# Batch-sized token groups, a ring for the GELU outputs, and a new order of all operations

## The chip, the cores and the metric

The kernel runs on one core of a Trainium2 chip. The time is what the device takes for one execution, in microseconds; before the change the median of three runs is 363.52 us (363.21 to 363.70).

## The reference

Squared-ReLU attention with 8 batches, 12 heads, 448 tokens and 64 elements per head is followed by a two-layer network over all 3584 tokens:

```python
scores = scale * np.matmul(q, k.transpose(0, 1, 3, 2))      # 1/sqrt(64)
attn = np.maximum(scores, 0.0) ** 2 / S
x = np.matmul(attn, v).transpose(0, 2, 1, 3).reshape(B * S, H * D)   # 3584 x 768
h = x @ w_in                                                 # 768 x 2048
g = h * (1.0 / (1.0 + np.exp(-1.702 * h)))                   # GELU
return (g @ w_out).astype(np.float32)                        # 2048 x 768
```

## The kernel before

Everything on the matrix engine is in float16 with float32 sums. The whole kernel is a list of some 1950 short words (lines 467 to 640), each of which issues one operation; `do` (line 441) translates them one after the other. The order of the words is the order of every engine's queue. Nothing else plans the work. A word is a letter, its indices, after `:` the engine (`a` ScalarE, `d` VectorE, `p` GpSimd), and after `@` the accumulator banks of PSUM that it takes. There are eight banks, each a pool of its own with one buffer, so a word that takes a bank waits until the last reader of that bank is done.

**Attention.** Four heads of a batch make a unit; there are 24 units, three to a batch. k and q of units 0 to 5 are brought in by GpSimd's queue (words `jk`, `jq`, which also narrow to float16) or by SP's (`Lk0`, `Lq0`) and turned around on TensorE (`tk`, `tq`, line 126, evacuated by `ek`, `eq`). Later units are loaded by SP (`Lk`, `Lq`), narrowed (`K`, `Q`) and turned around by a transposing DMA on SP's queue (`Rk`, `Rq`, line 117). v always comes over GpSimd's queue (`V`). A score word `s` (line 143) issues four quadrant products of 64 x 64 weights over 448 columns, and each unit has seven. Two ReLUs `r` and one square `x` follow it, on ScalarE or VectorE. When all seven are done, `a` (line 173) issues 28 quadrant products with v, and words `e` (line 189) copy the result into the transposed activations `xts`.

**First layer.** Tokens are taken in eight groups, `gblk = [6, 8] * 4` blocks of 64: 384 and 512 tokens in turn. Two batches of seven blocks make one pair of groups, so a batch's result is split between two groups, and `e` has pieces of 384, 64 and 448 columns. Group 0 is done plainly, by words `f` (line 221, two products each, 96 products in all) with GELU `g` and a widening `v` after it. The other groups use a scheme of seven products instead of eight (Strassen-Winograd) for each of four units of the 2048 hidden columns: words `u` (line 269, six products each, over half the group's tokens). `T` and `S` make the sums of activations and weights, `t` copies a first sum out of PSUM, `b` adds to it, `g` is the GELU and `v` the widening, mostly on GpSimd, into the outputs `gts`. These have one buffer for groups of even number (`ge`) and one for odd (`go`). The float32 tiles between `t` and `v` come from pool `gf`, which has five buffers.

**Second layer.** It works on tiles of 128 tokens. Two neighbouring tiles of a group make a pair, again with seven products instead of eight: words `p` (line 377), eight products of 384 columns each. `A` (line 357) makes the sums of activations, partly in place in `gts`; `W` made those of the weights once. `h` copies a partial result out, `l` adds the last part, `o` stores a tile in two pieces over SP's queue. A group of 512 tokens has two pairs. One of 384 has a pair and an unpaired tile, done by two words `i` (line 399, 16 products each) and copied out by `n`. Both of the last pair's tiles are stored in quarters by words `q`, on SP's and ScalarE's queues.

Before the first data arrive, 14 products with zeros run on TensorE (`z`), the first after two memsets on VectorE.

Of the kernel before, what the change touches and what calls it, by code (L numbers as in the profile page):

```python
# [15 lines left out]
def kernel(  # L16
# [22 lines left out]
    WO = 8  # L39

    gblk = [6, 8] * (B // 2)
    gcum = [0]
    for n in gblk:
        gcum.append(gcum[-1] + n)
    NG = len(gblk)
# [6 lines left out]
    for name, bufs in (("cst", 1), ("kst", 1), ("qst", 1), ("k16", 2), ("q16", 2), ("v16", 4),  # L52
                       ("kT", 3), ("qT", 3), ("at", 11), ("xe", 1), ("xo", 2),
                       ("T1", 1), ("T2", 1), ("T4", 1), ("ge", 1), ("go", 1), ("gf", 5),
                       ("as0", 1), ("as1", 1), ("osb", 3)):
        pool(name, bufs)
# [15 lines left out]
    wT = [const(f"wT{n}", [128, WO, NOUT]) for n in range(3)]  # L72

# [115 lines left out]
    def xt_evac(e, p, u, n, s):  # L189
        b, pr = divmod(u, NP)  # L190
        lo = b * J
        for _ in range(n + 1):
            g = max(i for i in range(NG) if gcum[i] <= lo)
            hi = min((b + 1) * J, gcum[g + 1])
            at, lo = lo, hi
        if g not in xts:
            xts[g] = new("xe" if g % 2 == 0 else "xo", [128, NK, 64 * gblk[g]], F16)
        copy(e, xts[g][:, 2 * pr + s, 64 * (at - gcum[g]):64 * (hi - gcum[g])],
             units[u]["av"][s][:, 64 * (at - b * J):64 * (hi - b * J)])
# [6 lines left out]
    gts = {}  # L206

    def gt_of(g):
        if g not in gts:
            gts[g] = new("ge" if g % 2 == 0 else "go", [128, NF, 64 * gblk[g]], F16)  # L210
        return gts[g]
# [9 lines left out]
    def m1(e, p, g, f, r):  # L221
        n = 64 * gblk[g]
        if r == 0:
            hp[g, f] = bank(p, "ht")
        w = win[f // WQ]
        fo = (f % WQ) * 128
        for i in (2 * r, 2 * r + 1):
            nc.tensor.matmul(out=hp[g, f][:, 0:n], lhsT=w[:, i, fo:fo + 128],  # L228
                             rhs=xts[g][:, i, 0:n], start=i == 0, stop=i == NK - 1)
# [3 lines left out]
    def m1_gelu(e, p, g, f):  # L233
        n = 64 * gblk[g]
        gfs[g, f] = new("gf", [128, 512], F32)
        gelu(gfs[g, f][:, 0:n], hp.pop((g, f))[:, 0:n])

    def m1_widen(e, p, g, f):
        n = 64 * gblk[g]
        widen(e, gt_of(g)[:, f, 0:n], gfs.pop((g, f))[:, 0:n])  # L240
# [11 lines left out]
    def x_block(g, kh, th):  # L252
        hn = 32 * gblk[g]
        return xts[g][:, kh * HK:(kh + 1) * HK, hn * th:hn * th + hn]
# [4 lines left out]
    def t_sum(e, p, g, n):  # L259
# [6 lines left out]
        xsum[g, n] = new(f"T{n}", [128, HK, 256], F16)[:, :, 0:32 * gblk[g]]  # L266
        tt(xsum[g, n], x, y, ALU.subtract, e)

    def unit_product(e, p, g, i, n):
        hn = 32 * gblk[g]  # L270
# [9 lines left out]
        for t in range(2):  # L280
            mm(hx[g, i, c][:, t * hn:(t + 1) * hn],
               lambda j: a[:, j, t * 128:(t + 1) * 128], lambda j: b[:, j, :], HK,
               n in (0, 1, 3) and t == 0)

    def half_of(x, g):
        return x[:, 0:64 * gblk[g]]

    def unit_snap(e, p, g, i, n):
        gfs[g, i, n] = new("gf", [128, 512], F32)
        copy(e, half_of(gfs[g, i, n], g), half_of(hx[g, i, 0], g))  # L290
# [4 lines left out]
    def unit_add(e, p, g, i, n):  # L295
        t = half_of(gfs[g, i, unit_tile[n]], g)
        tt(t, half_of(hx[g, i, 1], g), t, ALU.add)

    def unit_gelu(e, p, g, i, n):
        if n == 5:  # L300
            gfs[g, i, 5] = new("gf", [128, 512], F32)
            gelu(half_of(gfs[g, i, 5], g), half_of(hx[g, i, 0], g))
        else:
            t = half_of(gfs[g, i, unit_tile[n]], g)
            gelu(t, t)

    def unit_widen(e, p, g, i, n):
        fh, th = unit_place[n]
        hn = 32 * gblk[g]
        f = WQ * i + 2 * fh  # L310
        widen(e, gt_of(g)[:, f:f + 2, th * hn:(th + 1) * hn],
              half_of(gfs.pop((g, i, unit_tile[n])), g).rearrange("p (t c) -> p t c", t=2))
# [5 lines left out]
    def out_tile(g, m):  # L318
        if (g, m) not in osb:
            osb[g, m] = new("osb", [128, DM], F32)  # L320
        return osb[g, m]

    def store(e, p, g, m):
        t = osb.pop((g, m))
        for i in range(2):
            b, j = divmod(gcum[g] + 2 * m + i, J)
# [3 lines left out]
    def store_part(e, p, g, m, h, i):  # L330
        b, j = divmod(gcum[g] + 2 * m + i, J)
        r0 = b * S + j
        c = slice(h * NOUT, (h + 1) * NOUT)
        (nc.scalar if e == "a" else nc.sync).dma_start(
            out=out[r0:r0 + 63 * J + 1:J, c], in_=osb[g, m][64 * i:64 * i + 64, c])

    def m2(e, p, g, m, h):
        op[g, m, h] = bank(p, "op")
        mm(op[g, m, h][:, 0:NOUT], lambda f: gts[g][:, f, m * 128:(m + 1) * 128],
           lambda f: wout[h][f // WO][:, f % WO, :], NF, True)  # L340

    def m2_out(e, p, g, m, h):
        copy(e, out_tile(g, m)[:, h * NOUT:(h + 1) * NOUT], op.pop((g, m, h))[:, 0:NOUT], 1.0 / SC)
# [8 lines left out]
    def part(g, m, i):  # L352
        return gts[g][:, i * HF:(i + 1) * HF, m * 128:(m + 1) * 128]
# [3 lines left out]
    def a_sum(e, p, g, m, n):  # L357
        a11, a12 = part(g, m, 0), part(g, m, 1)
        if n == 5:
            sums[g, m, 5] = new(f"as{p.pop(0)}", [128, HF, 128], F16, "asum")  # L360
            tt(sums[g, m, 5], a11, a12, ALU.add, e)
            return
        a21, a22 = part(g, m + 1, 0), part(g, m + 1, 1)
        if n in (1, 2):
            sums[g, m, n] = new(f"as{p.pop(0)}", [128, HF, 128], F16, "asum")
        if n == 1:
            tt(sums[g, m, 1], a21, a22, ALU.add, e)
        elif n == 2:
            tt(sums[g, m, 2], sums[g, m, 1], a11, ALU.subtract, e)
        elif n == 3:  # L370
            tt(a21, a21, a11, ALU.subtract, e)
        else:
            tt(a12, a12, sums[g, m, 2], ALU.subtract, e)

    def pair_product(e, p, g, m, n):
        c = (0, 1, 0, 1, 0, 0, 1)[n]
        if n < 2:
            op[g, m, c] = bank(p, "ox")
        a = (lambda: part(g, m, 0), lambda: part(g, m, 1), lambda: sums[g, m, 2],
             lambda: sums[g, m, 1], lambda: part(g, m + 1, 0), lambda: part(g, m + 1, 1),  # L380
             lambda: part(g, m, 1))[n]()
        w = (wout[0][0], wout[0][1], wT[1], wT[0], wout[1][0], wT[2], wout[1][1])[n]
        mm(op[g, m, c][:, 0:NOUT], lambda f: a[:, f, :], lambda f: w[:, f, :], HF,
           n in (0, 1, 3))

    def pair_snap(e, p, g, m, n):
        i, c = {0: (0, lo), 2: (0, hi), 4: (1, hi)}[n]
        copy(e, out_tile(g, m + i)[:, c], op[g, m, 0][:, 0:NOUT], 1.0 / SC)

    def pair_last(e, p, g, m, n):  # L390
        i, c = {1: (0, lo), 3: (1, hi), 5: (1, lo), 6: (0, hi)}[n]
        o = out_tile(g, m + i)[:, c]
        if n == 5:
            copy(e, o, op[g, m, 0][:, 0:NOUT], 1.0 / SC)
        else:
            nc.vector.scalar_tensor_tensor(out=o, in0=op[g, m, 1][:, 0:NOUT], scalar=1.0 / SC,
                                           in1=o, op0=ALU.mult, op1=ALU.add)

    def single(e, p, g, m, h):
        op[g, m, h] = bank(p, "os")  # L400
        o = op[g, m, h][:, 0:NOUT]
        a1, a2 = part(g, m, 0), part(g, m, 1)
        s, t = ((a1, wout[0][0]), (a2, wout[0][1])) if h == 0 else (
            (a1, wout[1][0]), (sums[g, m, 5], wout[1][1]))
        mm(o, lambda f: s[0][:, f, :], lambda f: s[1][:, f, :], HF, True)
        mm(o, lambda f: t[0][:, f, :], lambda f: t[1][:, f, :], HF, False)
# [16 lines left out]
    with tc.manual_schedule():  # L423
        two = {"S": s_sum, "W": w_sum, "T": t_sum, "s": scores, "r": relu, "x": square,
               "e": xt_evac, "f": m1, "m": m2, "o": store, "u": unit_product,
               "t": unit_snap, "b": unit_add, "A": a_sum, "p": pair_product, "h": pair_snap,
               "l": pair_last, "i": single, "n": m2_out, "q": store_part, "jo": load_w_out, "a": attn_v,
# [24 lines left out]

        nc.vector.memset(warm, 0.0)
        nc.scalar.activation(out=warm, in_=warm, func=AF.Gelu_apprx_sigmoid)
        zero = wT[2][:, 0, :]
        nc.vector.memset(zero, 0.0)
        zp = []

        def zeros(e, p, n):
# [8 lines left out]
            "jq1 jk1 V0 z13@0 Lk0 K0:d z1 I tk0@1 Lq0 Q0:d jk3 ek0:a tq0@2 tq1@3 jq3 eq0 eq1 "  # L468
            "s0.1@4.5 r0.1.1 r0.1.0:d s0.4@6.7 r0.4.1:d jq2 s0.6@0.1 r0.6.0:d r0.4.0 V1 r0.6.1 "
            "s0.3@2.3 r0.3.1:d tk1@5 ek1:a s0.0@4.7 r0.0.0 x0.1 s1.4@0.6 r1.4.0:d r0.3.0 r1.4.1 "  # L470
            "s0.2@1.3 r0.0.1 r0.2.0:d s0.5@5.4 r0.5.1:d r0.2.1 r0.5.0 s1.1@0.2 jk2 x0.3 x0.2 "
            "s1.0@6.7 r1.0.1 x0.0 tk3@1 r1.1.1 r1.1.0 jwa0 jwb0 x0.5 x1.4 r1.0.0 s1.5@4.3 x0.4 jwb2 "
            "tq3@5 jq4 r1.5.1 s1.2@7.2 s1.6@0.6 r1.5.0 x1.0 x0.6:a eq3 jk4 V2 jwa2 a0@3.4 r1.6.1:d "
            "tk2@5 ek3 r1.6.0 ek2 x1.1:a tq2@6 eq2 r1.2.1 r1.2.0 e0.0.1:a s1.3@1.0 x1.2 x1.6 jwa1 "
            "r1.3.1 jwb1 s2.3@5.6 s2.1@2.7 e0.1.1:a r1.3.0 x1.3 x1.5 r2.3.0 jk5 jq5 r2.1.1:d e0.0.0 "
            "s2.2@0.4 r2.3.1 r2.2.0 r2.2.1 a1@1.5 s3.0@7.6 x2.3:a e1.0.0:a r2.1.0:d V3 s2.0@0.4 "
            "e1.1.0 r2.0.0 e0.1.0 s2.6@2.1 jwb3 r3.0.0:d r3.0.1 s2.4@0.3 r2.6.0:d f0.3.0@7 f0.2.0@6 "
# [193 lines left out]
```

## Time and profile before

| what | value |
|---|---|
| median of three runs | 363.52 us |
| the profiled execution's own time | 364.18 us |
| its span, first to last instruction | 362.4 us |
| TensorE busy | 352.5 us, 3598 products |
| VectorE busy | 309.1 us, 585 instructions |
| ScalarE busy | 284.9 us, 560 instructions |
| GpSimd busy | 111.8 us, 165 instructions |
| mean granted TensorE clock | 0.999 |
| DMA moved | 51.39 MB |

The page gives each engine's busy time, then the span in 40 slices with tenths of busy time, then the chain of work that ended last, followed back from the last instruction. Names like `hx<-win` are written tile and read tile: `sc` are scores, `av` attention results, `ht` and `hx` first-layer sums of group 0 and of the others, `ox` and `os` second-layer sums of pairs and of unpaired tiles, `tr` transposes, `zp` the zero products. Most products of both layers are issued by one helper (line 203), so that its line says little and the tile names say more. A line of the chain in order of time reads: start, length, engine and tile, and how many instructions were merged.

### The profile page before, as it was taken

The numbers are of one execution on the slowest core, as the hardware profiler recorded it, in microseconds if no ns is written. First come the engines' busy times: TensorE is split into PE (matmuls) and PEld (weight loads), VectorE is DVE, ScalarE is ACT, GpSimd is POOL, SyncE is SP. The second block draws the span as 40 slices with busy tenths as digits, with TensorE's granted clock in tenths as the row PEclk, the third lists the DMA queues.
The fourth block names the chain that finished last, engine by engine and source line by source line (L and its number), as shares of the span: only waits on it lengthen the run. The fifth ranks groups of instructions, "written<-read, shape, count | busy, mean of one in ns | idle before, by whom it ended". The sixth has DMA issues, their size and how long they took to land.

```text
span 362.4 us, 9114 instructions
## 1 busy us (share of the span) xinstructions
PE 352.5 (97%) x3598; PEld 236.0 (65%) x3598; DVE 309.1 (85%) x585; ACT 284.9 (79%) x560; POOL 111.8 (31%) x165
## 2 busy tenths in 40 slices
PE   8789999999999999999999999999999999999995
PEld 4445558855579555886569855786559855678662
DVE  3999999999997999888999799868999789875643
ACT  3999996999989997779996899878897697445420
POOL 5744522354225440155014440165021311001200
PEclk9999999999999999999999999999999999999999
DMA  8999999479999989535893764874590233003124
GB/s 182 173 200 201 215 231 228 107 149 220 196 209 189 241 158 260 165 110 79 203 213 77 216 81 118 147 152 104 115 171 4 47 110 89 2 0 89 44 67 110
DMA packets 65228, 51.39 MB, mean 142 GB/s; under 512 B 35744, under 2 KB 61856, under 8 KB 65184
## 3 DMA queue, kind: packets, MB, share of 16 engines
q1 hardware_dynamic: 48256, 36.32, 42.2%
q0 software_dynamic: 16608, 14.09, 27.0%
q8 instruction: 28, 0.46, 0.6%
q10 hardware_dynamic: 320, 0.39, 0.4%
q14 instruction: 16, 0.13, 0.1%
HBM read 45.61 MB, written 11.01 MB: 156 GB/s over the span
## 4 chain that ended last, share of the span: by engine, by line
PE 90%; DMA 5%; DVE 2%; POOL 1%; issue 0%; ACT 0%
PE hx L203 32%; PE ox L203 31%; PE sc L150 9%; PE av L181 8%; PE os L203 6%; DMA q<-in_q_dram 3%; PE ht L228 3%; DMA k<-in_k_dram 2%; PE zp L463 1%; PE tr L131 1%; DVE at L88 1%; POOL wout L415 0%; DVE at L161 0%; POOL q L104 0%; POOL v L104 0%
## 5 line engine op out<-in xcount | busy, mean ns | idle before, releaser
L163 ACT ACTIVATE at<-sc 128x448 f16<-128x448 f32 x218 | 108.2, 567 | 10.7 <-PE sc L150 9.9
L161 DVE TENSOR_SCALAR at<-sc 128x448 f16<-128x448 f32 x118 | 69.5, 614 | 3.6 <-PE sc L150 3.2
L203 PEld LDWEIGHTS <-win 128*128 128x128 f16 x672 | 61.5, 98 | 8.4 <-issue 1.8
L88 DVE TENSOR_TENSOR at<-at 128x896 f16<-128x896 f16 x109 | 65.9, 633 | 0.9 <-ACT at L163 0.2
L217 POOL TENSOR_SCALAR go<-gf 128x512 f16<-128x512 f32 x42 | 28.2, 671 | 109.9 <-ACT gf L214 108.3
L88 DVE TENSOR_TENSOR gf<-hx,gf 128x512 f32<-128x512 f32 (+1 forms) x84 | 51.6, 627 | 11.0 <-ACT gf L79 7.9
L214 ACT ACTIVATE gf<-gf 128x512 f32<-128x512 f32 (+1 forms) x84 | 47.5, 587 | 13.2 <-DVE gf L88 11.8
L169 ACT ACTIVATE at<-at 128x896 f16<-128x896 f16 x59 | 56.5, 974 | 1.1 <-DVE at L161 0.8
L217 POOL TENSOR_SCALAR ge<-gf 128x384 f16<-128x384 f32 x52 | 29.3, 563 | 73.3 <-ACT gf L214 60.8
L150 PE MATMUL sc<-qT,kT 64*64 64x448 f16 x672 | 48.9, 358 | 2.6 <-DVE qT L83 0.9
L203 PEld LDWEIGHTS <-winS 128*128 128x128 f16 x504 | 46.1, 98 | 5.5 <-issue 0.9
L79 ACT ACTIVATE gf<-hx 128x512 f32<-128x512 f32 (+1 forms) x63 | 34.5, 554 | 18.5 <-PE hx L203 15.0
L203 PE MATMUL ox<-wout,go 128*128 128x384 f16 x256 | 46.3, 326 | 0.0
L203 PEld LDWEIGHTS <-go 128*128 128x128 f16 x320 | 30.1, 98 | 22.0 <-issue 4.3
L203 PE MATMUL hx<-T,winS 128*128 128x256 f16 (+1 forms) x336 | 39.9, 261 | 0.0
L181 PE MATMUL av<-at,v 64*64 64x448 f16 x672 | 36.8, 350 | 0.9 <-ACT gf L214 0.6
L203 PEld LDWEIGHTS <-ge 128*128 128x128 f16 x256 | 24.0, 98 | 18.4 <-issue 4.5
L203 PE MATMUL hx<-xo,win 128*128 128x256 f16 x288 | 35.9, 273 | 0.0
L203 PE MATMUL ox<-wT,asum 128*128 128x384 f16 x192 | 34.9, 327 | 0.0
L150 PEld LDWEIGHTS <-kT 64*64 64x64 f16 x672 | 17.6, 105 | 24.7 <-issue 18.0
L203 PEld LDWEIGHTS <-asum 128*128 128x128 f16 x224 | 21.0, 98 | 15.7 <-issue 2.8
L181 PEld LDWEIGHTS <-v 64*64 64x64 f16 x672 | 20.3, 107 | 13.4 <-issue 2.9
(77 smaller groups left out, 452.2 us busy)
## 6 DMA issues: line engine op xcount, KB each, us to landing
out_dram<-osb SPq DMA_DIRECT2D x52, 192.0 KB, 3.9
kst<-in_k_dram SPq DMA_DIRECT2D x19, 448.0 KB, 4.5
qst<-in_q_dram SPq DMA_DIRECT2D x19, 448.0 KB, 4.3
v<-in_v_dram POOLq DMA_DIRECT2D x24, 224.0 KB, 5.5
win<-in_moe_w_in_dram POOLq DMA_DIRECT2D x8, 384.0 KB, 12.7
wout<-in_moe_w_out_dram POOLq DMA_DIRECT2D x4, 768.0 KB, 19.9
q<-in_q_dram POOLq DMA_DIRECT2D x5, 224.0 KB, 6.9
k<-in_k_dram POOLq DMA_DIRECT2D x5, 224.0 KB, 8.4
```

The costliest lines, as they stand in the source:

```text
L79: nc.scalar.activation(out=o, in_=i, func=AF.Copy)
L88: eng[e].tensor_tensor(out=o, in0=x, in1=y, op=op)
L131: nc.tensor.matmul(out=ps[64 * a:64 * a + 64, j * 128:(j + 1) * 128], lhsT=x[:, a, 64 * j:64 * j + 64], rhs=ident[:, :], is_transpose=True)
L150: nc.tensor.matmul(out=sc[a][c, 0:S], lhsT=st["kT"][r, j, c], rhs=st["qT"][r, :, c], start=True, stop=True)
L161: nc.vector.tensor_scalar(out=o, in0=i, scalar1=0.0, scalar2=None, op0=ALU.max)
L163: nc.scalar.activation(out=o, in_=i, func=AF.Relu)
L169: nc.scalar.activation(out=at, in_=at, func=AF.Square)
L181: nc.tensor.matmul(out=av[s][64 * a:64 * a + 64, 0:S], lhsT=v16[r, a, 64 * j:64 * j + 64], rhs=at[r, a, :], start=(j == 0), stop=(j == J - 1))
L203: nc.tensor.matmul(out=o, lhsT=lhs(i), rhs=rhs(i), start=start and i == 0, stop=i == n - 1, skip_group_check=True)
L214: nc.scalar.activation(out=o, in_=i, func=AF.Gelu_apprx_sigmoid, scale=1.0 / SC)
L217: eng[e].tensor_scalar(out=o, in0=i, scalar1=SC, scalar2=1.0, op0=ALU.mult, op1=ALU.mult)
L228: nc.tensor.matmul(out=hp[g, f][:, 0:n], lhsT=w[:, i, fo:fo + 128], rhs=xts[g][:, i, 0:n], start=i == 0, stop=i == NK - 1)
```

## The change

Token groups are now the eight batches, 448 tokens each, so `gblk`, `gcum` and the pieces of `e` go. An evacuation is one copy of 448 columns. The pools `xe`, `xo` become `xb` with two buffers, and the pool of squared scores `at` grows from 11 to 15 buffers.

The outputs of the first layer lie in one array, `ring`, of 2 x 448 tokens; group g writes its half g mod 2. The 28 tiles of 128 tokens are numbered through, tile m at column 128 x (m mod 7) of the ring, so that seven tiles fill it. The pairs are (0,1), (2,3) and so on to (26,27). Tiles 3, 10, 17 and 24 lie across the border of two batches, and pairs (6,7) and (20,21) have one tile in each of two batches. Unpaired tiles, their words `i`, `n`, and the fifth sum of `A` are gone. In the last pair, products 3 and 6 can be done in two halves of 192 columns, in banks of their own, with their additions and the final stores halved as well.

All words are ordered anew, from the first to the last. There are 16 opening products with zeros instead of 14, and the memset that they need comes ahead of the other one.

```diff
-    gblk = [6, 8] * (B // 2)
...
+    HS = S // 2
...
-                       ("kT", 3), ("qT", 3), ("at", 11), ("xe", 1), ("xo", 2),
-                       ("T1", 1), ("T2", 1), ("T4", 1), ("ge", 1), ("go", 1), ("gf", 5),
+                       ("kT", 3), ("qT", 3), ("at", 15), ("xb", 2),
+                       ("T1", 1), ("T2", 1), ("T4", 1), ("gf", 5),
...
+    ring = const("ring", [128, NF, 2 * S])
...
+    def xt_evac(e, p, u, s):
         b, pr = divmod(u, NP)
...
+        if b not in xts:
+            xts[b] = new("xb", [128, NK, S], F16)
+        copy(e, xts[b][:, 2 * pr + s, :], units[u]["av"][s][:, 0:S])
...
     def gt_of(g):
-        if g not in gts:
-            gts[g] = new("ge" if g % 2 == 0 else "go", [128, NF, 64 * gblk[g]], F16)
-        return gts[g]
+        return ring[:, :, S * (g % 2):S * (g % 2) + S]
...
-    def part(g, m, i):
-        return gts[g][:, i * HF:(i + 1) * HF, m * 128:(m + 1) * 128]
+    def part(m, i):
+        c = 128 * (m % J)
+        return ring[:, i * HF:(i + 1) * HF, c:c + 128]
...
+    def pair_product(e, p, m, n, h=None):
+        c = (0, 1, 0, 1, 0, 0, 1)[n] if h is None else 2 + h
+        if n < 2 or (n == 3 and h is not None):
+            op[m, c] = bank(p, "ox")
...
+        k = quarter(h)
+        mm(op[m, c][:, k], lambda f: a[:, f, :], lambda f: w[:, f, k], HF, n in (0, 1, 3))
...
-    def single(e, p, g, m, h):
...
-        nc.vector.memset(warm, 0.0)
-        nc.scalar.activation(out=warm, in_=warm, func=AF.Gelu_apprx_sigmoid)
         zero = wT[2][:, 0, :]
         nc.vector.memset(zero, 0.0)
+        nc.vector.memset(warm, 0.0)
+        nc.scalar.activation(out=warm, in_=warm, func=AF.Gelu_apprx_sigmoid)
...
-            "jq1 jk1 V0 z13@0 Lk0 K0:d z1 I tk0@1 Lq0 Q0:d jk3 ek0:a tq0@2 tq1@3 jq3 eq0 eq1 "
-            "s0.1@4.5 r0.1.1 r0.1.0:d s0.4@6.7 r0.4.1:d jq2 s0.6@0.1 r0.6.0:d r0.4.0 V1 r0.6.1 "
...
+            "z9@0 z1 z1 jq1 z1 z1 jk1 V1 I Lq0 Lk0 z1 z1 z1 Q0:d tq0@1 eq0:a K0:d tk0@2 tq1@3 ek0 "
+            "eq1 s0.5@4.5 jq2 r0.5.1:d r0.5.0 s0.1@6.7 jk2 s0.2@0.1 r0.2.1 r0.1.1:d jq3 s0.0@2.3 "
...
-            "q7.2.0.1:a h7.2.4 l7.2.3 q7.3.1.0 A7.2.4 q7.3.1.1:a l7.0.6 p7.2.5 l7.2.5 p7.2.6 "
-            "q7.3.0.1:a o7.0 q7.3.0.0 l7.2.6 q7.2.1.1:a q7.2.1.0"
+            "q26.0.0 l26.3.1 q26.0.1:a l26.3.0 q27.1.0 q27.1.1:a l24.6 o24 p26.5 l26.5 p26.6.0 "
+            "l26.6.0 p26.6.1 q27.0.1:a q27.0.0 q26.2.0 q26.2.1:a l26.6.1 q26.3.0 q26.3.1:a"
```

## The prediction

> **What bounds the kernel now.** I read the page's busy shares first, then its chain of work, then that chain in order of time, then engine sums for three stretches, then the last instructions.
>
> ```profile
> span 362.4 us, 9114 instructions
> PE 352.5 (97%) x3598; PEld 236.0 (65%) x3598; DVE 309.1 (85%) x585; ACT 284.9 (79%) x560; POOL 111.8 (31%) x165
> ...
> PE   8789999999999999999999999999999999999995
> ...
> DMA  8999999479999989535893764874590233003124
> ...
> PE 90%; DMA 5%; DVE 2%; POOL 1%; issue 0%; ACT 0%
> ```
>
> The chain is TensorE for 90% of the span. A busy TensorE need not stream at its peak, so I take the price of each product from the chain in order of time:
>
> ```profile
> 124.52 0.50 PE sc L150 x8
> 125.02 1.32 PE av L181 x28
> 126.72 2.71 PE ox L203 x16
> 129.43 0.69 PE sc L150 x12
> ...
> 188.48 1.49 PE hx L203 x18
> ...
> 324.24 4.58 PE hx L203 x42
> ...
> 342.52 15.61 PE ox L203 x96
> ```
>
> Columns are start, length, what. A product of 384 columns takes 15.61/96 = 162.6 ns, one of 256 columns 4.58/42 = 109.0 ns, one of 192 columns 1.49/18 = 82.8 ns. The three lie on one line: 0.417 ns per column and about 2.5 ns per product, so 224 columns cost 95.8 ns and 448 cost 189 ns. Two score words (x8) take 0.50 us, three 0.69, so a word is 0.19 us and the first has 0.12 more. Two second-layer products after scores take 2.71 us where 16 x 0.1626 is 2.60. A switch between quadrant products (scores, attention times v) and full-array products thus costs 0.11 us on either side.
>
> ```profile
> 6.70:52.60 45.90, 41.43 (x562) 23.63 (x560) 43.38 (x84) 43.21 (x91) 23.81 (x34) 1.00 1.26 201
> 10.00:39.30 29.30, 25.26 (x352) 13.93 (x351) 28.25 (x58) 28.06 (x61) 16.42 (x23) 1.00 1.26 193
> 52.60:358.12 305.52, 305.52 (x3014) 209.44 (x3014) 263.60 (x497) 240.19 (x469) 84.95 (x122) 1.00 0.62 132
> ```
>
> Columns: stretch, length, busy us of TensorE, weight loads, VectorE, ScalarE, GpSimd, granted clock, DMA share, GB/s. From 52.6 to 358.12 TensorE never idles. With the prices above, its words and switches from `a5` on (the attention product that starts at 52.5) come to 303.9 us against the 305.6 that passed: real stalls there are under 2 us. Before 52.6 it is otherwise: VectorE and ScalarE are busy 96% of 10 to 39.3, TensorE loses time, and DMA is full (the page's nines up to some 63 us). So the kernel is a head set by VectorE, ScalarE and loads, a body set by TensorE alone, and a tail:
>
> ```profile
> 357.62 1.58 SPq L334 DMA_DIRECT2D out_dram<-osb  x2
> 358.15 0.56 DVE L396 SCALAR_TENSOR_TENSOR osb<-ox,osb 128x384 f32<-128x384 f32 x1 [0.74 <-PE ox L203]
> ```
>
> After the last product come one 0.56 us addition and 3.7 us of store.
>
> **The change, part by part.**
>
> *Second layer.* Four unpaired tiles of 32 products each (128) become two pairs of 56 (112): 16 products of 384 columns fewer, 16 x 162.6 = -2.60 us. In the last pair two products are cut into halves, 16 of 384 columns into 32 of 192: 32 x 82.8 - 16 x 162.6 = +0.05.
>
> *First layer of group 0.* 96 plain products grow from 384 to 448 columns: 96 x (189.2 - 162.6) = +2.55 us.
>
> *First layer, other groups.* 672 products of 256 columns and 504 of 192 (73.2 + 41.7 = 114.9 us) become 1176 of 224 (112.7): -2.2 us. Here a rule speaks against the change. The row: a weight load reads 98 ns, and yet 192-column products come every 82.8 ns, so loads go on beside products. The Trainium skill, "TensorE: Matmul & The Clock Gate", section "LDWEIGHTS (loading the stationary operand)", prices a load at its columns over 1.2, 107 ns for 128, and the section "Back-to-back issue gap" lets both loads and products set the spacing. If 107 were the floor, 224-column products would cost 107: 1176 x 107 = 125.8 against 672 x 109 + 504 x 107 = 127.2, -1.4 instead of -2.2, and the halved last pair +0.8 instead of +0.05. The row decides, as it shows spacings below that floor; the rule's sum, 1.6 us worse, stays in the range.
>
> *Switches.* Counted in the two orders: 106 before, 109 after, +0.3. Opening zero products 14 to 16: 2 x 0.16 = +0.3 if they run at the later rate (they run at 0.32 each at first, so up to +0.6).
>
> TensorE's own sum: -2.60 + 0.05 + 2.55 - 2.2 + 0.3 + 0.3 = **-1.6 us**, all of it on the path that sets the end.
>
> *Other engines.* Row means times counts: VectorE 345.9 to 343.4 us, ScalarE 338.4 to 339.8, GpSimd 112 to 117. (Consecutive instructions overlap, so the busy sums are 0.89 and 0.84 of these.) Copies of attention results fall from 72 to 48; paired output adds and fewer plain output copies about balance. None comes near TensorE's body time. Those edits cost nothing while TensorE covers them; uncovered, the ScalarE surplus is 1.4 x 0.84 = 1.2 us.
>
> *The head, by the new order.* Work placed ahead of `a5`: TensorE before 42 score words 7.9, 5 attention products 6.6, 44 group-0 words 14.3, transposes 6.9, zeros 2.3, one unit word 0.7, switches 1.6: 40.2. After: 43 group-0 words of 2 x 189 = 16.3, two unit words 1.2, zeros 2.6, switches 1.8, rest alike: 43.3. ScalarE before 58 ReLUs x 0.567, 8 squares x 0.974, 12 GELUs and 12 copies: 54.4; after 57 ReLUs, 10 squares, 13 wider GELUs, 9 copies, one cast: 56.2. VectorE 51.5 to 52.1. ScalarE's 54.4 x 0.84 + 6.7 (its first real work) = 52.5 is just when `a5` starts now, so ScalarE paces the head. After: 56.2 x 0.84 + 6.7 = 54.0, and TensorE has 299.2 us left from there instead of 303.9. Its end moves by +1.5 - 4.7 = -3.2, of which -1.6 is the sum above and **-1.6 the head**. If VectorE paced it instead, `a5` would come at 53.1 and the head give -2.5; if loads do, nothing. GpSimd's queue keeps its loads (24 v, 10 q and k, 12 weights); cast loads are full there now, `V0` falls from third to eighth, behind `jk3`, which waits for transposes of unit 1. Its landing (8 pieces deep, as `jk2` was, which landed at 18.3) and the work ahead of `a0` (ScalarE 14.5 x 0.84 + 6.7 = 18.9) meet: a loss of 0 to 1 us. I take -1.2 for the head.
>
> *SP's queue.* Same 38 loads, 36 transposing loads and 52 stores, and one final piece more (one more on ScalarE's too, at the very end). Transposing loads stood as little as 0.2 us of TensorE work ahead of their first scores; in the new order the least is 3.3. No new wait expected.
>
> *The ring.* Outputs of group g+2 overwrite those of g, as with the single buffers before, but now seven tiles share two groups. GpSimd's widenings that also wait for TensorE rise from 4 to 13 of 94; behind such a one stand the next casts and widenings, and behind those ScalarE's GELUs, which need the five `gf` buffers. No row shows the wait. Bounds: nothing (each is ordered behind the product it waits for), or 13 x 0.62 (a widening's length) = 8 us. I take +0.4, near the lower end, since the body has under 2 us of stalls now with the same kinds of waits.
>
> *Tail.* The last addition covers 192 columns, about half of the 0.56 us, and the last pieces are half as large: -0.3 (0 to -0.6).
>
> **Sum.** -1.6 - 1.2 + 0.4 - 0.3 = -2.7. The profiled span becomes 362.4 - 2.7 = 359.7. That execution took 364.18 (1.78 around the span), 0.66 above the runs' median of 363.52; a difference carries over, so 363.52 - 2.7 = **360.8 us**.
>
> **Rivals.**
>
> *Loads set the head.* DMA is full there and its order hardly changes. The head then gives 0, with up to 1 us lost on `V0`: -1.6 - 0.3 + 0.4 + 0.5 = -1.0, 362.5 us. Against it: in the view of waits only 0.9 us of TensorE's idle time ends on a load.
>
> *The head gives all,* paced by VectorE, no new stalls: -1.6 - 2.5 - 0.3 = -4.4, 359.1 us. For it: VectorE and ScalarE are equally busy there.
>
> *Seams stall TensorE: slower.* Six pairs now hold tokens of two batches and can't finish until the later batch's first half has passed all four units: addition 0.62, GELU 0.58, widening 0.62, two sums of 0.69, 3.2 us from the last unit product to the pair's third product. If TensorE had nothing else, that were 6 x 3.2 = 19 us. With 1 us lost at each seam the sum is -2.7 + 6 = +3.3, 366.8 us. It is slower than before from 0.45 us per seam. Against it: the order places 11.7 to 19.7 us of other TensorE work there, and 5.8 us at the last.
>
> **How the numbers follow.** The sum 0.52, the full head 0.23, loads in the head 0.13, seams 0.12. A measurement tells about 0.2%, 0.7 us, from no change. Faster by more: the first two, and 0.05 of the third, where `V0` costs nothing: 0.80. Within 0.2%: the rest of the third, 0.08. Slower: the seams, 0.12. The range reaches from the full head with the far end of the tail, 359.1 - 0.3 = 358.8, to the loads case with the weight-load rule beside it, 362.5 + 1.6 = 364.1.
>
> **What would show it.** Group 0's products at 189 ns; unit products at 95.8, or 107 if the rule holds; no unpaired tiles; `a5` near 54 us; no TensorE idle after it; the last product near 355. It is wrong if TensorE idles between a unit's last product and a seam pair's, if ScalarE waits for GpSimd's widenings, or if `a0` waits for its v.

## The result, and the profile after

The changed kernel takes 362.58 us (median of 16 runs, 361.75 to 363.69), the kernel before 363.61 us beside it (16 runs, 362.33 to 365.33). The ratio is 0.9973, 95% interval 0.9958 to 0.9987: faster by about 1.0 us, where 2.7 were forecast. The profiled execution took 363.36 us.

From the page of the changed kernel: busy shares, the slices of TensorE and DMA, and the chain that ended last.

```profile
span 361.6 us, 9118 instructions
PE 351.8 (97%) x3600; PEld 240.6 (67%) x3600; DVE 313.2 (87%) x578; ACT 286.0 (79%) x551; POOL 116.9 (32%) x169
...
PE   8799999999999999999999999999999999999995
...
DMA  8999999679889999868699625980381101130314
...
PE 85%; DMA 6%; DVE 4%; ACT 2%; POOL 2%; issue 1%; POOLq 0%
```

The span fell only from 362.4 to 361.6, and the chain now leaves TensorE for 15% of the span instead of 10%. The shares alone show no more than that. The prices come next, then the places where TensorE fell behind.

The chain in order of time of the changed kernel (start, length, what):

```profile
45.07 2.00 PE ht L214 x10
...
50.52 2.65 PE ht L214 x14
...
232.97 8.05 PE hx L194 x84
...
338.94 18.25 PE ox L194 x128
```

A 448-column product costs 2.65/14 = 189 ns and a 224-column product 8.05/84 = 95.8 ns, both as forecast. The last row, 96 products of 384 columns and 32 of 192, is 18.25 us where 96 x 0.1626 + 32 x 0.0828 = 18.26. Group 0 has 96 products and the unpaired tiles are gone.

To see where time was lost I use one number per word. A word's *arrear* is its start in the trace less the price of all TensorE words and switches ordered ahead of it. It grows only where TensorE loses time. All prices add up to 344.07 us before and 342.47 after, the forecast -1.6.

| profiled execution | before | after | difference |
|---|---|---|---|
| all TensorE prices | 344.07 | 342.47 | -1.60 |
| arrear at `a5` (head) | 12.30 | 10.74 | -1.56 |
| arrear gained from `a5` to `a23` (body) | 1.54 | 3.76 | +2.22 |
| last product to the end of the span | 4.28 | 4.40 | +0.12 |
| sum (what lies after `a23` is equal to 0.02) | | | -0.82 |

So the prices came as forecast and the head as its full value, and the body gave more than half of it back. These are two single executions; how far each part wanders from one execution to the next is said below. The same stretches in the table of engine sums (stretch, length, busy us of TensorE, weight loads, VectorE, ScalarE, GpSimd, clock, DMA share, GB/s), first after:

```profile
6.70:54.05 47.35, 44.00 (x572) 23.36 (x569) 45.53 (x83) 44.10 (x89) 27.18 (x36) 1.00 1.21 199
54.05:357.18 303.13, 302.25 (x3011) 214.63 (x3010) 265.80 (x491) 240.38 (x461) 86.65 (x124) 1.00 0.63 132
...
90.00:100.00 10.00, 9.70 (x120) 5.02 (x118) 10.00 (x19) 10.00 (x21) 1.87 (x2) 1.00 0.90 201
120.00:130.00 10.00, 9.65 (x107) 5.27 (x106) 9.61 (x17) 9.65 (x20) 3.30 (x5) 1.00 0.81 168
```

and the kernel before:

```profile
90.00:100.00 10.00, 10.00 (x96) 5.33 (x94) 9.37 (x18) 9.95 (x21) 2.85 (x5) 1.00 0.97 193
120.00:130.00 10.00, 10.00 (x116) 5.51 (x108) 9.35 (x19) 9.56 (x18) 2.48 (x5) 1.00 1.08 271
```

From 90 to 100 us VectorE and ScalarE have no free moment at all (10.00 of 10.00) and TensorE idles 0.3 us. The arrear grows in few places: `p0.6` 0.36 us (at 83.5 us), `p2.0` 0.21, `s8.0` 0.60 (at 93.2), `p2.2` 0.26, `s9.1` and `p2.3` 0.25 together, `p4.3` 0.57 (at 130.2), `p6.4` 0.15, `u4.0.5` 0.19. A busy TensorE row hides part of this, as `a7` at 91.26 shows beside `a6` at 85.34 in the timeline of the changed kernel:

```profile
85.34 1.49 PE L178 MATMUL av<-at,v 64*64 64x448 f16 x28
...
90.34 1.15 DVE L85 TENSOR_TENSOR at<-at 128x896 f16<-128x896 f16 x2
90.48 1.44 ACT L160 ACTIVATE at<-sc 128x448 f16<-128x448 f32 x3
...
91.26 2.11 PE L178 MATMUL av<-at,v 64*64 64x448 f16 x28
...
91.76 0.99 ACT L166 ACTIVATE at<-at 128x896 f16<-128x896 f16 x1
...
93.18 0.57 PE L147 MATMUL sc<-qT,kT 64*64 64x448 f16 x8
```

28 products that wait for nothing fill a row of 1.49 us, as `a6`'s do (28 times 47 ns, and the modelled end of the last). `a7`'s take 2.11: in the middle they wait for the square of tile 5 of unit 7 (91.76 to 92.75 on ScalarE), which stands in ScalarE's queue behind ReLUs of the next unit. At `p4.3` it is VectorE:

```profile
127.00 1.10 POOL L80 CAST k<-kst 128x896 f16<-128x896 f32 x1 [3.00 <-DMA kT<-k]
127.22 1.35 DVE L85 TENSOR_TENSOR at<-at 128x896 f16<-128x896 f16 x1
...
129.03 0.61 DVE L85 TENSOR_TENSOR at<-at 128x896 f16<-128x896 f16 x1
...
129.56 0.55 DVE L366 SCALAR_TENSOR_TENSOR osb<-ox,osb 128x384 f32<-128x384 f32 x1
...
130.16 1.14 PE L194 MATMUL ox<-wT,asum 128*128 128x384 f16 x6 [0.51 <-DVE osb L366]
```

The addition `l4.1` (129.56) must free its bank before `p4.3` can write it, and from 127.22 on it stands behind a square, a ReLU and a square. The first square took 1.35 us instead of 0.61: a GpSimd cast was under way when it started, and the square ended 0.48 us after the cast (128.57 and 128.09). That alone is 0.74 us, more than the 0.57 us of the wait. Where the square starts first, the cast is the one that is held up:

```profile
85.91 0.62 DVE L85 TENSOR_TENSOR at<-at 128x896 f16<-128x896 f16 x1
...
85.95 1.36 POOL L80 CAST k<-kst 128x896 f16<-128x896 f32 x1
```

The same cast met a square in this way, 1.35 us, in 14 of the 16 profiles of the changed order. In one of the other two the square was left out.

No wait of TensorE in the list leads to the ring. GpSimd's widenings, which write it, waited for one thing, the GELU's output from ScalarE (waits: us in total, times, longest):

```profile
POOL ring L204 <- ACT gf L201: 152.7, 55, 18.9
```

ScalarE in turn waited for widenings 3.4 us in all, and 3.9 in the kernel before.

The tail, additions and issues of the last stores on SP's and ScalarE's queues:

```profile
356.48 2.13 SPq L313 DMA_DIRECT2D out_dram<-osb  x3
356.49 2.04 ACTq L313 DMA_DIRECT2D out_dram<-osb  x3
...
357.22 0.36 DVE L366 SCALAR_TENSOR_TENSOR osb<-ox,osb 128x192 f32<-128x192 f32 x1 [0.23 <-PE ox L194]
```

The last addition takes 0.36 us instead of 0.56, as forecast, and ends at 357.58. But both queues are still issuing earlier pieces; the last pieces are issued there at 357.96 and 357.99, 0.4 us later. In the kernel before the last two were issued at 358.74 and 358.75, when the addition had ended at 358.71.

### The profile page after: what moved, and what is told of

Same layout as the page of the kernel before. It is cut to its first block, busy times and chain, and to the rows that moved or that the text cites. A ratio compares the mean times of both kernels' runs of the same rounds, so it can differ in the third digit from the quotient of the medians.

```text
span 361.6 us, 9118 instructions
## 1 busy us (share of the span) xinstructions
PE 351.8 (97%) x3600; PEld 240.6 (67%) x3600; DVE 313.2 (87%) x578; ACT 286.0 (79%) x551; POOL 116.9 (32%) x169
## 4 chain that ended last, share of the span: by engine, by line
PE 85%; DMA 6%; DVE 4%; ACT 2%; POOL 2%; issue 1%; POOLq 0%
PE ox L194 34%; PE hx L194 32%; PE sc L147 8%; PE av L178 7%; DMA k<-in_k_dram 3%; DMA q<-in_q_dram 3%; PE ht L214 3%; PE zp L424 1%; DVE at L85 1%; DVE at L158 1%; POOL ring L204 1%; ACT at L160 1%; ACT gf L201 1%; PE tr L128 0%; DVE asum L85 0%
## 5 line engine op out<-in xcount | busy, mean ns | idle before, releaser
L204 POOL TENSOR_SCALAR ring<-gf 128x448 f16<-128x448 f32 x94 | 58.0, 617 | 156.1 <-ACT gf L201 152.7
L194 PE MATMUL ox<-wout,ring 128*128 128x384 f16 (+1 forms) x456 | 80.3, 324 | 0.1
L194 PEld LDWEIGHTS <-ring 128*128 128x128 f16 x568 | 53.7, 98 | 35.9 <-issue 6.1
L85 DVE TENSOR_TENSOR gf<-hx,gf 128x448 f32<-128x448 f32 x84 | 51.1, 620 | 10.8 <-PE hx L194 4.9
L201 ACT ACTIVATE gf<-gf 128x448 f32<-128x448 f32 x84 | 46.8, 573 | 15.1 <-DVE gf L85 14.9
L194 PE MATMUL hx<-xb,win 128*128 128x224 f16 x504 | 58.0, 259 | 0.0
L76 ACT ACTIVATE gf<-hx 128x448 f32<-128x448 f32 x59 | 31.4, 542 | 13.2 <-PE hx L194 9.5
L194 PE MATMUL ox<-wT,asum 128*128 128x384 f16 (+1 forms) x232 | 41.0, 321 | 0.7 <-DVE osb L366 0.5
L194 PE MATMUL hx<-T,winS 128*128 128x224 f16 x336 | 39.7, 259 | 0.0
L366 DVE SCALAR_TENSOR_TENSOR osb<-ox,osb 128x384 f32<-128x384 f32 (+1 forms) x44 | 23.3, 533 | 8.9 <-PE ox L194 6.9
```

Source lines behind the costliest of these rows:

```text
L76: nc.scalar.activation(out=o, in_=i, func=AF.Copy)
L85: eng[e].tensor_tensor(out=o, in0=x, in1=y, op=op)
L194: nc.tensor.matmul(out=o, lhsT=lhs(i), rhs=rhs(i), start=start and i == 0, stop=i == n - 1, skip_group_check=True)
L201: nc.scalar.activation(out=o, in_=i, func=AF.Gelu_apprx_sigmoid, scale=1.0 / SC)
L204: eng[e].tensor_scalar(out=o, in0=i, scalar1=SC, scalar2=1.0, op0=ALU.mult, op1=ALU.mult)
L366: nc.vector.scalar_tensor_tensor(out=o, in0=x, scalar=1.0 / SC, in1=o, op0=ALU.mult, op1=ALU.add)
```

## Experiments

Two first ideas for the lost 2.2 us. Theory 1: ScalarE and VectorE are busy nearly everywhere, so what TensorE gains earlier is swallowed by them later. Theory 3: the waits are fixed by the new order and move along with TensorE. The first expectations also weigh a theory 2, that the waits hang on the ring and the seams. The numbers at experiments are ratios to the kernel before on the same chip, with 95% intervals; arrears are from each profile. Times of kernels run beside each other can be compared to some 0.5 us, the arrears far more closely: in 16 profiles of the changed order, wherever nothing near was edited, the wait at `p0.6` was 0.35 to 0.38 us, at `p2.0` 0.21 to 0.22, at `s8.0` 0.60 to 0.62 and at `p4.3` 0.57 to 0.60. Other parts wander: `a5` starts between 53.2 and 55.1 us without any edit ahead of it, and the last product is 4.3 to 4.8 us from the end in the twelve profiles with an unedited tail.

**A delay at the head.** Extra products ahead of `f0.13.0`, 1.5 us, in both kernels; their sums are overwritten.

```diff
+        if (g, f, r) == (0, 13, 0):
+            for _ in range(8):        # 9 of 384 columns in the kernel before
+                nc.tensor.matmul(out=hp[g, f][:, 0:S], lhsT=w[:, 0, fo:fo + 128],
+                                 rhs=xts[g][:, 0, 0:S], start=True, stop=True, ...
```

> The changed kernel with 8 more products of 448 columns (8 x 0.189 = 1.5 us of TensorE alone) in front of the first-layer word f0.13.0, at about 54 us; their sums are overwritten. Theory 1, busy engines: TensorE, which now comes out of the head 1.6 us earlier, is held up at 82 to 98 and at 129 us by VectorE and ScalarE, which are busy without a gap there; so most of the 1.5 us is swallowed: the end moves by +0.0 to +0.6, and the waits at 82 to 130 shrink by about 1 us or more. Theory 2, ring and seams: the waits hang on pairs over a border of two batches, whose inputs come from TensorE's own products; everything shifts and the end moves by +1.5. Theory 3, fixed chains: the waits are latencies of this order, whenever TensorE comes: +1.5 as well.

> The kernel before with 9 more products of 384 columns (9 x 0.1625 = 1.5 us) in front of its word f0.13.0, at about 51 us. It has only some 0.7 us of waits between 52 and 143 us. Theory 1: not more than those 0.7 us can be swallowed, so the end moves by +0.8 to +1.5, more than in the changed kernel. Theories 2 and 3: +1.5, as in the changed kernel.

After: 364.64 us, ratio 1.0017 (0.9998 to 1.0035), 0.44% or 1.6 us above the changed kernel's ratio. The body's arrear grew by 3.50, as without the delay (3.50 in most profiles; 3.76 in the first one, where `u4.0.5` and `p2.2` waited longer). The arrears show that none of the 1.5 us was swallowed, and theory 1 falls as it was put. Before: 366.52 us, 1.0077 (1.0050 to 1.0104), 2.8 us for a delay of 1.5. In its profile, which at 368.75 us is slower than the median, the body's waits are up from 1.54 to 3.79. The expectation, at most 1.5, missed this. What stalled there was not pursued; it shows that the order before isn't robust either when TensorE comes late.

**Squares left out.** 14 squares of units 7, 8, 10 and 11 (10 on VectorE, 4 on ScalarE), or 14 of units 17, 19 and 20; those scores go on unsquared.

```diff
     def square(e, p, u, j):
         at = ats.pop((u, j))
         slots[u, j] = at
+        if (u, j) in (...):
+            return
```

> The changed kernel without 14 squares (10 on VectorE, 4 on ScalarE, 10 us of engine time in all) of units 7, 8, 10 and 11, whose attention falls into 80 to 100 and 120 to 141 us; those scores go on unsquared. TensorE's work is the same. Theory 1: its waits at 82 to 98 and at 130 us vanish and the end comes 1.2 to 2.0 us earlier, 360.6 to 361.4. Theories 2 and 3: the waits stay, the end moves by 0 to -0.3.

> The same as the run with the dense squares left out, but for 14 squares (10 on VectorE, 4 on ScalarE) of units 17, 19 and 20, at 225 to 270 us, where TensorE hardly waits. All three theories: no change, within 0.3 us of the changed kernel; if it is faster by 1 us, load on VectorE or ScalarE matters all over the body and theory 1 is too narrow.

The first: 361.59 us, 0.9929 (0.9903 to 0.9955); the body's waits 2.50. The waits at `p2.0`, `p2.2`, `s9.1`, `p2.3` and `p4.3` all but vanished; that at `s8.0` stayed (0.67), as its square was not among the 14. The second: 363.18 us, 0.9984 (0.9968 to 0.9999), waits 3.50, unchanged. Load on VectorE and ScalarE counts from 82 to 131 us, and not at 225 to 270. Theories 2 and 3 as they were put, with waits that stay, fall by the first. One of the 14 squares is the one that met the GpSimd cast. The engine sums of the first kernel show it:

```profile
90.00:100.00 10.00, 9.87 (x121) 5.07 (x119) 8.37 (x16) 8.65 (x18) 1.87 (x2) 1.00 0.81 214
120.00:130.00 10.00, 10.00 (x113) 5.07 (x114) 7.84 (x15) 9.55 (x20) 2.92 (x4) 1.00 0.84 164
```

**The head.** Five of ScalarE's squares (units 1, 2, 4) left out, with the same edit.

> The changed kernel without 5 squares of ScalarE (4.7 us of its time) in units 1, 2 and 4, at 14 to 45 us. If ScalarE paces the head, a5 comes earlier by 1 us or more. Theory 1, busy engines: a good part of what the head gains is given back between 80 and 143 us, so the end moves by less than half of what a5 moves. Theories 2 and 3: the end moves by as much as a5. If loads pace the head, a5 stays at 54.0.

362.80 us, 0.9982 (0.9971 to 0.9993). `a5` came at 52.76 us, arrear 9.45, waits 3.50. Five squares are 5 x 0.974 x 0.84 = 4.1 us of ScalarE, while `a5`'s arrear fell by 1.1 against the unedited head, whose arrear ranges from 9.88 to 11.77 over 15 profiles with a median of 10.57. So ScalarE is not the head's only pacer. What the head gained was not given back in the body; in the measured time no gain can be told.

**The tail.** First with the last pair's products whole, then with halves but the second half of tile 26 stored at once:

```diff
-"... q26.2.0 q26.2.1:a l26.6.1 q26.3.0 q26.3.1:a"
+"... l26.6.1 q26.1.0 q26.1.1:a"
```

> The changed kernel with the last pair's products, additions and stores whole again, as before the change. My prediction's step for the tail: +0.3 us. Rival, from the profile after: the final pieces queue behind each other on SP and ScalarE (each issue takes 0.47 to 0.79 us), so that halving gained at most 0.15: 0 to +0.2.

> The changed kernel with the halved products and additions kept, but the two last stores of tile 26's second half as whole pieces behind the last addition (two issues fewer, 96 KB instead of 48 KB each). If the queue of issues eats what halving gains, the last issue starts at the end of the last addition instead of 0.4 us later: -0.2 to -0.4. If the size of the last pieces counts: 0 or later.

Whole: 362.43 us, 0.9973 (0.9962 to 0.9985), tail 4.12. Merged: 362.44 us, 0.9968 (0.9956 to 0.9980), tail 3.87. The first has no halves, and its tail is no longer than the changed kernel's 4.3 to 4.8: halving products and stores gained nothing. The issues show why: 0.2 us saved by the shorter addition, 0.4 lost until the last pieces are issued. With the issues merged the tail is 3.87, and 4.37 and 3.99 in two later kernels with the same tail; the measured time doesn't show a gain.

**More work to GpSimd.** GpSimd is busy 32%; nine casts and widenings of VectorE and ScalarE (`Q11`, `K12`, `K14`, `v1.2.3`, `v1.3.3`, `v2.1.5`, `v2.1.6`, `v2.2.6`, `v2.3.6`) were given to it in place.

> The changed kernel with nine operations (two q casts or k casts on VectorE and one on ScalarE, six widenings on VectorE; about 4.5 us of their time) moved to GpSimd, most of them due between 85 and 145 us, where GpSimd is busy less than half of the time. Nothing is left out. Theory 1: TensorE's waits shrink, -0.5 to -1.5 us. Theories 2 and 3: nothing, or slower, since a widening takes 0.62 us there instead of 0.42.

365.38 us, 1.0061 (1.0037 to 1.0086): slower. The waits up to `a11` were the same as before the move (2.56 and 2.55). Then some 5 us were lost by 157 us, in a profile (368.03 us) slower than the median. In this kernel's waits of VectorE and of TensorE from 140 to 160 us:

```profile
DVE asum L85 <- POOL ring L204: 5.0, 1, 5.0
...
PE hx L194 <- DVE xb L85: 2.6, 1, 2.6
```

`v2.3.6` stood in GpSimd's queue behind the cast `Q16`, which waited for its load until 149.68 us (in the changed kernel until 148.77, but there VectorE does `v2.3.6` itself); the sum `A8.1` waited for the widening, and VectorE's whole queue waited behind it. An engine at 32% is free on average and was blocked when it was needed.

**Single words moved.** First the late square `x7.5` to GpSimd and `l4.1` ahead of a square on VectorE; then this with the merged tail; then, without GpSimd, both words moved within their own queues, with the merged tail. The changed kernel ran again beside the second.

```diff
-"... s8.3@5.4 r8.1.1 x7.5:a r8.3.0 ..."
+"... x7.5:p K11:p s8.3@5.4 r8.1.1 r8.3.0 ..."     # first and second
+"... s8.3@5.4 x7.5:a r8.1.1 r8.3.0 ..."           # third
...
-"... r10.6.0:d x10.5 s11.1@2.4 ... Lk14 l4.1 r11.2.1 ..."
+"... r10.6.0:d l4.1 x10.5 s11.1@2.4 ... Lk14 r11.2.1 ..."
```

> The changed kernel with two words moved, nothing left out: square x7.5 from ScalarE (where it stands behind six ReLUs of unit 8, and the attention product a7 waits for it) to GpSimd, ahead of its cast K11; and the addition l4.1 ahead of square x10.5 in VectorE's queue, as product p4.3 waits for l4.1. If the waits in the body are fixed chains, single words standing behind others in a queue, both waits vanish (0.6 us in a7 to s8.0, 0.57 us at p4.3) and the end moves by -0.9 to -1.2. If what counts is the sum of VectorE's and ScalarE's work there, 1 us less on ScalarE gives -0.0 to -0.4, and the order on VectorE gives nothing.

> The two moves and the merged last stores together. If both add up: the moves' gain and 0.4 to 0.7 us more from the tail, -1.4 to -1.8 against the changed kernel, so 360.8 to 361.2 and 0.992 to 0.993 of the kernel before. If the tail is worth nothing: the same as the two moves alone.

> The changed kernel itself, beside the other two on the same chip, as their measure: 0.9973 of the kernel before again, 0.996 to 0.999. In its profile the waits from a5 to a23 add up to 3.5 us, as in every variant whose order is the same there, whatever the head took.

> The changed kernel with two words moved within their own engines' queues and a shorter tail: the square of unit 7's tile 5 on ScalarE goes ahead of the ReLU before it, the addition of pair 4's second product on VectorE goes ahead of the square before it (no GpSimd work is added), and the last two quarters of tile 26's second half are stored whole. Theory 3 (waits are fixed by single words that stand too late in a queue): the wait at the scores of unit 8 (0.60 us, at 93 us) falls below 0.2, the wait at pair 4's fourth product (0.57 us, at 130 us) below 0.1 with at most 0.3 coming back later, the other waits stay within 0.05; the body's waits fall from 3.5-3.8 to 2.6-3.0, the tail from 4.4 to 3.9; time 1.0 to 1.2 us below the changed kernel, ratio about 0.994 to the kernel before. If the stretches are short of the engines' throughput (the sum over ScalarE and VectorE, not the order of two words, decides), the waits come back at the next words: body waits 3.4 or more, ratio 0.9960 to 0.9975 (the tail alone).

The first: 364.52 us, 1.0014 (1.0002 to 1.0026); the second 363.87, 0.9992 (0.9975 to 1.0009); the changed kernel 362.75, 0.9966 (0.9951 to 0.9981). The changed kernel's waits were 3.9 here and not the 3.5 expected: 0.4 came at `p14.3`, near 231 us, just after a square on VectorE that took 1.34 us beside a GpSimd cast. The move to GpSimd made it worse: the wait at `s8.0` grew from 0.60 to 1.44 and at `p2.2` to 0.89. In the timeline of the first:

```profile
89.19 2.19 POOL L85 TENSOR_TENSOR at<-at 128x896 f16<-128x896 f16 x1 [1.05 <-ACT at L160]
...
90.29 2.83 DVE L85 TENSOR_TENSOR at<-at 128x896 f16<-128x896 f16 x2
...
91.33 1.32 POOL L80 CAST k<-kst 128x896 f16<-128x896 f32 x1
...
93.18 0.95 PE L178 MATMUL av<-at,v 64*64 64x448 f16 x16 [0.89 <-DVE at L85]
```

The square takes 2.19 us on GpSimd, and pushes the cast `K11` behind it into the second of the two squares that VectorE does at the time. These take 2.83 us together, where the changed kernel's row at 90.34 has 1.15 for the same two. The first ends 0.48 us after GpSimd's square (91.38), the second 0.48 us after the cast (92.64).

The third: 362.41 us, 0.9962 (0.9950 to 0.9975), the lowest ratio of a kernel that computes everything, but not separable from the changed kernel. The square was no longer waited for, `s8.0` fell from 0.60 to 0.16, and then the next two words waited: `s8.6` 0.31, for the ReLU that the square had displaced, and `p2.2` 0.15, together 0.62. `p4.3` fell from 0.57 to 0.03, and `p4.5` waited 0.33. The waits came back by all of the first and half of the second; the body's waits were 3.3 in all, between the two forecasts. The order of two words is then not the whole cause. The reading that follows from it is that the stretch is short of ScalarE's and VectorE's time; the next expectations call it the stretch theory. The square ahead of `p4.3` still met the GpSimd cast in this run and took 1.35 us, so for that wait the collision stays a rival.

**TensorE work put into the stretch.** If so, TensorE work added there should cost nothing. Four more products of 384 columns (0.65 us) ahead of `p2.1` and of `p4.1`, or, as a control, ahead of `p14.1` and `p18.1`:

```diff
+        if (m, n) in ((2, 1), (4, 1)):         # control: (14, 1), (18, 1)
+            for _ in range(4):
+                nc.tensor.matmul(out=op[m, c][:, k], lhsT=a[:, 0, :], rhs=w[:, 0, k],
+                                 start=True, stop=True, skip_group_check=True)
```

> The changed kernel with 8 products of 384 columns more on TensorE (their sums are overwritten): four ahead of pair 2's second product (at 89 us) and four ahead of pair 4's (at 126 us), 2 x 0.65 = 1.3 us of TensorE work placed just ahead of the two longest waits of the body (0.60 us at 93 us, 0.57 us at 130 us). Stretch theory (ScalarE and VectorE are asked for more there than they serve in TensorE's time): the added work fills the waits, which fall from 0.60 and 0.57 to under 0.1 each; the end moves by 0.2 to 0.5 us; ratio about 0.9980 to the kernel before. Fixed waits (the two engines fall back with TensorE as they did when the delay lay in the head): waits stay, the end moves by 1.3 us or more; ratio about 1.0005.

> The same 8 products at two places without waits, ahead of pair 14's second product (at 226 us) and of pair 18's (at 293 us). Stretch theory and fixed waits both say that nothing takes them in: the end moves by 1.3 us; ratio about 1.0005. If they cost 0.5 us or less here too, the result of the other run is no sign of dense stretches.

Dense: 363.49 us, 1.0005 (0.9987 to 1.0023). Control: 364.05 us, 1.0008 (0.9995 to 1.0020). The times speak for fixed waits: both lie near their 1.0005, and 0.9980, the stretch theory's, lies outside the first interval. The arrears are mixed: from `a5` to `a14` they grew by 2.54, in the control by 2.92. The gain is all in one place. At `p4.3` the wait went from 0.57 to nothing; 0.20 came at `u2.1.2`, which the control doesn't have. In this run, though, two squares came ahead of the GpSimd cast and only a later one was held up, to 0.82 us, so that the lost wait is no clean sign of time filled. At `s8.0` the wait stayed 0.55. There the added work stood ahead of score words `s8.1` and `s8.3`, whose ReLUs stand ahead of the awaited square, and so delayed both sides alike. The control kept all its waits. For the last run the first four products of `a7` were done four times (12 more, 0.56 us), behind those score words, and the four ahead of `p4.1` were kept:

```diff
-        for j in range(J):
+        for i, j in enumerate([0] * (3 if u == 7 else 0) + list(range(J))):
```

> The changed kernel with TensorE work added only between score words and the word that waits: unit 7's attention product repeats its first four products three times (12 x 47 ns = 0.56 us, overwritten) behind the scores whose ReLUs stand ahead of the square that it waits for, and pair 4's second product keeps its four extra products (0.65 us) ahead of the wait at 130 us. 1.21 us more on TensorE. Stretch theory, refined (ScalarE and VectorE need longer from a score word to the word that waits for it than TensorE has work between them; work between fills the wait, work ahead of the scores moves both): waits at 93 us (0.60) and 130 us (0.57) both fall under 0.1, the body's waits from 3.5 to about 2.4, the end moves by 0.1 to 0.3 us; ratio about 0.9975. Fixed waits: the end moves by 1.2 us, ratio about 1.0003.

> The changed kernel as it is, beside the other run on the same chip: ratio 0.9966 to 0.9973 as before, body waits 3.5 to 3.9.

363.49 us, 0.9998 (0.9983 to 1.0012), beside 362.99, 0.9980 (0.9967 to 0.9993), for the changed kernel. In time this is again what fixed waits forecast (1.0003), with the stretch theory's 0.9975 outside the interval. In the timeline `a7` now holds 40 products, which need 1.89 us:

```profile
90.71 2.35 PE L178 MATMUL av<-at,v 64*64 64x448 f16 x40
```

where 28 took 2.11 in the changed kernel. The waits are 0.12 at `s8.0` and none at `p4.3`; from `a5` to `a14` the arrear grew by 1.89 against 2.90 in the run beside it. The square ahead of `p4.3` took 1.35 us here too. So in the arrears up to `a14` 1.0 of the 1.21 us of added work filled waits. The end did not show it, since a wait of 0.78 us appeared at `u4.0.5`, near 200 us, described below. The run before with work added in the stretch has a wait of 1.20 at the same word, the only other long one there. Whether the added work brought them on, so that it was paid for after all, was not tested.

## Why the prediction was partly right

**Right: TensorE's own sum**, -1.6: prices 344.07 to 342.47. **The row against the rule:** 224-column products come every 95.8 ns and 192-column ones every 82.8. The floor of 107 ns that the prediction made of the load's price in the Trainium skill's "TensorE: Matmul & The Clock Gate", section "LDWEIGHTS (loading the stationary operand)", did not show; the page prices the load and names no such floor.

**Right in size: the head.** `a5` was forecast "near 54 us" and came at 54.05; the head gave -1.56 where -1.2 was taken and -1.6 was the full value. That the two agree so closely is luck. That ScalarE alone paces it is not shown: with 4.1 us of its work gone the head moved by about 1 us, and without any edit `a5` wanders over 1.9 us from profile to profile. `V0`'s later landing cost nothing that shows.

**Wrong: "I take +0.4, near the lower end, since the body has under 2 us of stalls now with the same kinds of waits."** The body's waits rose by 2.2. The term was sized by the ring, and no wait of TensorE led to the ring. The mistake lies one step earlier: *"None comes near TensorE's body time. Those edits cost nothing while TensorE covers them."* That compares sums over 300 us. The new order packs attention more tightly in some stretches. From `a6` to `a8` the words ordered on TensorE need 9.9 us at their prices (14.8 before). ScalarE's words there are 19 ReLUs, 3 squares, 3 attention copies and an output copy, (19 x 0.582 + 3 x 0.969 + 3 x 0.592 + 0.492) x 0.84 = 13.6 us; before they were 15, 7, 5, 2 and a GELU, (15 x 0.567 + 7 x 0.974 + 5 x 0.535 + 2 x 0.496 + 0.6) x 0.84 = 16.4 us. ScalarE's demand went from 1.11 to 1.37 times TensorE's; VectorE's, summed in the same way, from 1.00 to 1.14 times. A demand above TensorE's is no wait by itself, as the order before shows with 1.11 and hardly a stall; work queued up ahead covers part of it, and by this account TensorE waits for the rest. What the runs showed in its place: the body's waits rose by 2.2 us, and they stand at words that wait for squares on ScalarE and for sums and additions on VectorE. Load taken out of the two engines removes 1.0 us of them. TensorE work put between the scores and the waiting word fills 1.0 of 1.21 us up to `a14`, though not in the measured time. In the changed order neither an earlier nor a later TensorE changes them.

The stretch account does not carry over to `p4.3`. From `a9` to `a11`, around that wait, ScalarE is asked for 14.4 us and VectorE for 14.8, and TensorE for 15.6. The collision of a square with a GpSimd cast is enough for that wait, and the prediction gave GpSimd's work no cost on other engines. No run took the cast away, so that its share is argued from the rows, and how much of the 2.2 us is VectorE's and how much ScalarE's was not separated either.

**Wrong by a smaller amount: "SP's queue ... No new wait expected."** In 3 of the 16 profiles of the changed order TensorE waited at `u4.0.5`, near 200 us, 0.19, 1.20 and 0.78 us. There ScalarE's cast of q of unit 20 waits for a transposing load to finish with the buffer it writes, and the copy that TensorE needs stands behind the cast. In the run with 40 products:

```profile
197.93 0.95 ACT L76 ACTIVATE q<-qst 128x896 f16<-128x896 f32 x1 [1.22 <-DMA qT<-q]
...
199.63 0.52 ACT L76 ACTIVATE gf<-hx 128x448 f32<-128x448 f32 x1
...
200.20 0.73 PE L195 MATMUL hx<-T,win 128*128 128x224 f16 x6 [0.61 <-ACT gf L76]
```

The prediction counted how early transposing loads stand before their scores, and not which casts wait for them.

**Wrong: the tail**, -0.3 forecast, +0.1 between the two profiles and no gain in the others. The addition is shorter, as said, but the last pieces were costed by their size and not by their issue: six issues on two queues take about 2.1 us, and the last two came 0.4 us after the addition.

**The rivals.** The case "loads set the head" named 362.5 us, close to the result, for a reason that did not hold: the head did give its gain. Seams did not stall TensorE in the way feared. Seam pair 2 did wait, 0.21, 0.26 and 0.13 us at `p2.0`, `p2.2` and `p2.3`, and pair 6 waited 0.15 at `p6.4`. But the widening that pair 2 needs ended at 85.9 us and its first sum began only at 89.2, when VectorE came to it. The second was itself held up by a GpSimd cast, 0.92 us instead of 0.68:

```profile
91.92 0.93 POOL L80 CAST k<-kst 128x896 f16<-128x896 f32 x1 [3.73 <-DMA kst<-in_k_dram]
...
92.48 0.92 DVE L85 TENSOR_TENSOR asum<-asum,ring 128x1024 f16<-128x1024 f16 x1
...
93.68 1.31 PEld L194 LDWEIGHTS <-asum 128*128 128x128 f16 x8 [0.33 <-DVE asum L85]
```

## What to carry over

Check cover stretch by stretch: for each stretch of the order, sum what is asked of every engine and compare it with what the bounding engine has *there*; a busy share over the whole span hides a stretch of ten microseconds where another engine is asked for more. The sum is a sign and not a proof: 1.11 cost nothing here. When a wait is found, look first whether one operation ahead of it took longer than its kind does elsewhere, and what ran beside it. Moving the one late word tells little, because the next word waits in its place; taking work off the engine that is late tells more. An engine that is idle most of the time is no safe place for work when its queue holds an operation that waits for a load.

## What the runs showed of the hardware

- A square on VectorE and an operation on GpSimd hold each other up, and the one that starts first keeps its time. A square that started 0.22 us into a GpSimd cast took 1.35 us instead of 0.61 and ended 0.48 us after the cast (rows at 127.00 and 127.22). The two at 90.29 also ended 0.48 us after the GpSimd operation beside each. A square that started ahead of a cast kept its 0.62 us, and the cast took 1.36 instead of 0.93 (rows at 85.91 and 85.95). The Trainium skill, "SBUF — State Buffer", section "Who interferes with whom", describes a port pair that the two engines share under an exclusive lock, so that whichever issues first blocks the other fully; the rows agree.
- The same square takes 0.61 us on VectorE, 0.99 on ScalarE and 2.19 on GpSimd.
- The delay of 1.5 us in the kernel before cost 2.8 us; in the changed kernel it cost 1.6.
